# Token sums: where the first combined operands, the Relus and GpSimd's weight sums are put

## Chip, cores and metric

The kernel runs on one core of one Trainium2 chip. The metric is device time in microseconds (us). Everything is float32.

Engines are named as in the profile: PE is TensorE (matmuls; PEld its weight loads), DVE is VectorE, ACT is ScalarE, POOL is GpSimd, SP is SyncE, which here only issues DMAs. PSUM is the memory that PE writes to, in banks; SBUF holds everything else on the chip.

## What is computed

The input x has 8 images of 3008 tokens by 256 channels. A filter over the tokens is followed by a mixer over tokens and then over channels.

```python
X = np.fft.rfft(x, axis=1)
x = np.fft.irfft(X * (filt_r + 1j * filt_i)[None], n=3008, axis=1)      # filter
xt = x.transpose(0, 2, 1)
h = np.maximum(xt @ w_tok1, 0.0) @ w_tok2                               # 3008 -> 256 -> 3008
u = x + h.transpose(0, 2, 1)
h2 = np.maximum(u @ w_ch1, 0.0) @ w_ch2                                 # 256 -> 1536 -> 256
return u + h2
```

## The kernel before

**The loop.** `mix` goes through the mixer's work in 288 steps: 8 images `b`, 6 stretches of tokens `m` in each (512 tokens wide, the last 448), 6 channel pairs `jp` in each stretch. So an image has 36 steps, `i % n` from 0 to 35 with n = 36, and a step is one channel pair of one stretch. A step multiplies up to the hidden channels (`up_first`, `up_middle`, `up_last`) and, one step behind, down from them (`h_sums`, `down`). Between these, at three places of a step, come other pieces: token products for the next image, parts of `u` for the next stretch (`u_parts`), and, through the generator's yields, the filter of images that come later (`dft`, L523 on PE and L674 to L680 on DVE in its second half).

**Order.** The schedule is written by hand. Each engine works through its instructions in the order in which the program issues them, and so does each engine that issues DMAs: SP and POOL also keep the order of their DMAs. What stands earlier in the code on one engine is done earlier there.

**Seven products for eight.** All large products are done by a scheme that replaces eight block products by seven, with sums of the blocks ahead of and behind them. Weights therefore come as seven blocks: four of them raw or nearly so, others sums that `combine` forms on POOL (L378 to L382). On the side of the data, sums of the four blocks are formed on DVE: `h_sums` and `u_sums` for the channel part (tiles `t` and `v`), `t4_sums` for the token part (tile `ts`). The helper `v` issues every DVE sum, so they all carry its line, L910, and are told apart by their tiles.

**Token product.** For images 1 to 7, `token_product` (L802 on PE) forms the first token product from the filtered rows in `t4`. It runs over 12 pairs of row groups. In a pair there are 7 products, each of which is two passes on PE, into two PSUM banks called `one` and `two` (`ps_acc` and `ps_b` in the trace). Three use raw rows, four use sums in `ts`. `ts` holds two pairs of four 128 x 128 sums, so the sums of pair j + 2 are formed after pair j's products. It stands in step 32 of an image (the `n - 4` of the code), at the last of its three places, and belongs to the next image. The sums of pairs 0 and 1 are formed earlier in that step, after one piece of the delayed work of the preceding stretch (`one_step`; here it is an output transpose and the output's DMAs on POOL).

Behind the products, the same function forms the results in a tile `c`: a copy on ACT (L808), five sums on DVE, two Relus on ACT into `h1` (L815), and `combine` of `h1` on POOL. PE first uses `h1` in step 34.

**Up, in a step.** `up_first` issues four products, into four half banks, and a copy `s` of the first of them by ACT (L935). `up_middle` is two sums on DVE that read `s` and the banks, into `hh` and `s`. `up_last` issues three more products into half banks that these two sums have read, then two sums and two Relus (L953).

**Weight sums on POOL.** The weights of the token product are loaded and converted for image 0 into `w1` and used once as they are. For the later images, `w1_sums` then makes the seven blocks from them: `raw_out` stores the raw ones to DRAM by two POOL DMAs (L761, L762; 0.77 and 1.54 MB by their KB in the profile), sixteen POOL sums of 128 x 384 (L765) overwrite `w1` in place, and `sums_out` stores the four sums (L774). A list `w1_todo` holds these 18 pieces; `mix` takes two from it in each step from step 8 of image 0. `w2_sums` does the same for the second token weight (L880 to L896), one piece a step, also from step 8.

**Other work on POOL and SP in image 0.** In the first steps of image 0 the last channel weights are still converted on DVE, and `combine` finishes them on POOL (`wc`). Up to step 7 the first transform of images 1 and 2 is done (L530 on PE), with results stored through ACT's queue to `z_tmp`. At the second place of step 7, three POOL memsets clear the tiles `filt` (L694); then SP loads the filter's rows into `filt` and the transform's results into `t` (`t<-z_tmp`), in this order in its queue, and the first filter product (L523) follows in step 8.

## Time and profile before

| | us |
|---|---|
| median of 3 runs | 2470.65 (2469.56 to 2470.77) |
| profiled execution, own time | 2472.55 |
| its span, first to last instruction | 2470.8 |
| PE busy | 2409.5 (98%) |
| DVE busy | 1946.4 (79%) |
| ACT busy | 687.0 (28%) |
| POOL busy | 622.1 (25%) |

How to read it: the profile is of one execution; its span leaves out what lies around the first and the last instruction. Matmuls are pipelined and their ends are modelled, so a busy PE is not PE at its peak. POOL's 622.1 us are for the most part the issue of output DMAs (L1013, 409.6 us). In lines of the timeline the first two numbers are the start (us from the span's start) and the time from the first to the last of the merged instructions; then engine, line, operation, tiles written and read, and in brackets the idle time before it and what ended it. In lines of the waits: who waited, for whom, total us, times, longest.

### The profile page before, as it was taken

What the parts mean: (1) busy time and instruction counts of PE and PEld (TensorE: products, weight loads), DVE (VectorE), ACT (ScalarE), POOL (GpSimd) and SP (SyncE); (2) the same over time, 40 slices, a digit from 0 to 9 for tenths busy, and PEclk for the clock granted to TensorE, in tenths of its full rate; (3) what the DMA queues carried; (4) which work ended last, traced back from release to release, by engine and by line L of the source; (5) the groups of instructions that cost most, each with busy time, mean ns of one, the idle gap of its engine ahead of it and who ended that gap; (6) DMA issues with size and microseconds to landing.
All of it is one profiled execution on the core that took longest, in us unless ns stands there. A gap on an engine that the chain in (4) does not pass through costs nothing.

```text
span 2470.8 us, 35576 instructions
## 1 busy us (share of the span) xinstructions
PE 2409.5 (98%) x12340; PEld 1969.5 (80%) x12340; DVE 1946.4 (79%) x3684; ACT 687.0 (28%) x1355; POOL 622.1 (25%) x1110
## 2 busy tenths in 40 slices
PE   7999999999999999999999999999999999999998
PEld 4667666978878787987888878897888888898887
DVE  7797878787887888778877887877787788777776
ACT  5733222133221222123221222213221222212222
POOL 8473632113111211211121112112212112112121
PEclk8999999999999999999999999999999999999999
DMA  9974455453442322435334222433324121411100
GB/s 217 239 230 150 142 159 176 151 158 113 120 139 87 86 83 79 157 108 167 99 115 128 86 70 81 155 93 116 98 82 147 50 71 46 148 62 29 40 14 20
DMA packets 187339, 278.65 MB, mean 113 GB/s; under 512 B 35405, under 2 KB 125211, under 8 KB 187160
## 3 DMA queue, kind: packets, MB, share of 16 engines
q1 hardware_dynamic: 140952, 212.56, 28.4%
q0 software_dynamic: 34608, 53.83, 8.1%
q10 hardware_dynamic: 11600, 10.00, 1.3%
q8 instruction: 98, 1.61, 0.3%
q14 instruction: 81, 0.66, 0.1%
HBM read 193.52 MB, written 82.72 MB: 112 GB/s over the span
## 4 chain that ended last, share of the span: by engine, by line
PE 84%; DVE 9%; DMA 3%; issue 1%; ACT 1%; POOL 0%; SPq 0%; DVEq 0%; ACTq 0%
PE ps_po L966 31%; PE ps_pg L932 18%; PE ps_pg L948 13%; PE ps_b L523 4%; PE ps_b L802 3%; PE ps_acc L853 3%; PE ps_acc L802 2%; PE ps_b L853 2%; DVE t L910 2%; PE ps_b L831 2%; PE ps_acc L831 2%; DVE hh L910 2%; DMA st<-in_moe_w_tok_dram 1%; PE ps_acc L523 1%; DVE s L910 1%
## 5 line engine op out<-in xcount | busy, mean ns | idle before, releaser
L1013 POOL DMA_DIRECT2D out_dram<-r x752 | 409.6, 553 | 1623.3 <-ACT hh L953 1341.0
L910 DVE TENSOR_TENSOR hh<-ps_pg,s 128x512 f32<-128x512 f32 (+3 forms) x864 | 482.5, 586 | 240.0 <-ACT s L935 236.1
L953 ACT ACTIVATE hh<-hh 128x512 f32<-128x512 f32 (+1 forms) x576 | 348.0, 622 | 966.9 <-DVE hh L910 966.9
L966 PE MATMUL ps_po<-t,wc 128*128 128x256 f32 (+1 forms) x2304 | 548.2, 381 | 6.2 <-DVE t L910 4.4
L966 PEld LDWEIGHTS ps_po<-t,wc 128*128 128x128 f32 x2304 | 425.0, 190 | 136.1 <-DVE t L910 49.8
L966 PE MATMUL ps_po<-hh,wc 128*128 128x256 f32 (+1 forms) x1728 | 414.0, 375 | 1.4 <-POOL wc L382 0.8
L932 PE MATMUL ps_pg<-v,wc 128*128 128x256 f32 (+1 forms) x1728 | 413.4, 375 | 0.1
L966 PEld LDWEIGHTS ps_po<-hh,wc 128*128 128x128 f32 x1728 | 326.5, 190 | 42.7 <-ACT s L935 3.9
L932 PEld LDWEIGHTS ps_pg<-v,wc 128*128 128x128 f32 x1728 | 326.9, 190 | 40.6 <-DVE v L910 2.6
L948 PE MATMUL ps_pg<-u,wc 128*128 128x256 f32 (+1 forms) x1152 | 296.0, 379 | 6.0 <-DVE hh L910 6.0
L948 PEld LDWEIGHTS ps_pg<-u,wc 128*128 128x128 f32 x1152 | 214.3, 190 | 65.7 <-DVE hh L910 32.7
L910 DVE TENSOR_TENSOR t<-t,hh 128x256 f32<-128x256 f32 (+1 forms) x576 | 247.2, 429 | 19.8
L910 DVE TENSOR_TENSOR s<-ps_pg,hh 128x512 f32<-128x512 f32 (+1 forms) x288 | 196.1, 681 | 30.7 <-DVE hh L910 0.9
L935 ACT COPY s<-ps_pg 128x256 f32<-128x256 f32 (+1 forms) x288 | 105.9, 368 | 327.9 <-PE ps_pg L932 325.3
L910 DVE TENSOR_TENSOR t<-hh 128x512 f32<-128x512 f32 (+1 forms) x288 | 196.1, 681 | 0.6 <-ACT hh L953 0.6
L932 PE MATMUL ps_pg<-u,wc 128*128 128x256 f32 (+1 forms) x576 | 172.3, 381 | 3.9 <-DVE hh L910 3.9
L948 PE MATMUL ps_pg<-v,wc 128*128 128x256 f32 (+1 forms) x576 | 168.8, 375 | 0.0
L932 PEld LDWEIGHTS ps_pg<-u,wc 128*128 128x128 f32 x576 | 105.8, 190 | 36.8 <-DVE hh L910 21.8
L910 DVE TENSOR_TENSOR u<-ps_acc,u 128x256 f32<-128x256 f32 (+1 forms) x84 | 46.2, 550 | 94.0 <-PE ps_acc L853 86.4
L948 PEld LDWEIGHTS ps_pg<-v,wc 128*128 128x128 f32 x576 | 108.8, 190 | 13.0
L910 DVE TENSOR_TENSOR u<-ps_b,u 128x512 f32<-128x512 f32 (+2 forms) x126 | 74.5, 591 | 28.8 <-PE ps_b L853 26.7
L853 PE MATMUL ps_acc<-w 128*128 128x256 f32 (+1 forms) x336 | 85.2, 376 | 0.0
(149 smaller groups left out, 2744.6 us busy)
## 6 DMA issues: line engine op xcount, KB each, us to landing
w<-w_tmp SPq DMA_DIRECT2D x84, 448.0 KB
w<-w_tmp SPq DMA_DIRECT2D x35, 896.0 KB
out_dram<-r POOLq DMA_DIRECT2D x696, 32.0 KB, 3.1
t<-g_tmp SPq DMA_DIRECT2D x42, 512.0 KB
g_tmp<-t SPq DMA_DIRECT2D x96, 192.0 KB
t<-z_tmp SPq DMA_DIRECT2D x180, 96.0 KB
z_tmp<-t SPq DMA_DIRECT2D x60, 256.0 KB
filt<-in_x_dram SPq DMA_DIRECT2D x90, 128.0 KB
```

Of the source, the lines that this page charges most:

```text
L523: nc.tensor.matmul(outs(i, j), stat(i, j), mov(i, j), start=True, stop=True)
L802: nc.tensor.matmul(ps[:, at], w[:, n], mov, start=(j == 0 and i in (0, 2)), stop=(j == AP - 1 and i >= 5))
L831: nc.tensor.matmul(ps[:, ds(q * P, n)], t4[b, c][:, r, ts(dh, P)], wai[:, 0:n], start=(first and q == 0), stop=(not first and q == 3))
L853: nc.tensor.matmul(ps[:, ds(j * hw, hw)], h1[:, n, :], w2m[m % 2][:, at, 0:hw], start=(i < 2 and j == 0), stop=(j == len(todo) - 1))
L910: nc.vector.tensor_tensor(out=out, in0=in0, in1=in1, op=op)
L932: nc.tensor.matmul(ps[:, 0:hw], chan[0][:, jp, n, :], mov, start=True, stop=True)
L935: nc.scalar.copy(out=s[:, 0], in_=g[0][:, 0, 0:hw])
L948: nc.tensor.matmul(ps[:, 0:hw], chan[0][:, jp, n, :], mov, start=True, stop=True)
L953: nc.scalar.activation(out=hs, in_=hs, func=AF.Relu)
L966: nc.tensor.matmul(po[i][:, j, 0:hw], chan[1][:, jp, n, :], mov, start=(jp == 0 and first == 1), stop=(jp == JP - 1 and last == 1))
L1013: q.dma_start(bass.AP(tensor=ob.tensor, offset=ob.offset + row * D + g * cw, ap=[[N1 * D, 32], [D if h else -D, n], [1, cw]]), blocks[ts(g ...
```

## The change

1. In `token_product` the seven products of a pair stand in another order: the three with raw rows come first, the four with sums after them. In `mix`, `t4_sums` of pair 0 moves ahead of the delayed piece of work in step 32; that of pair 1 stays behind it.
2. The last of the five sums, the two Relus and `combine` of `h1` become a function that is put aside, and is called in the next step, after `up_first` and `up_middle`.
3. `w1_todo` is taken from at the start of a step: one piece (`raw_out`) in step 4 of image 0, six in each of steps 5, 6 and 7 (the sixth to the eighth channel pair). Nothing is left for step 8 and later.

No instruction is added or taken away.

```diff
-    token_ts = {}
+    token_ts, todo_h1 = {}, []
...
-            todo = ((one, 0, 0, rows[:, 0]), (one, 3, 6, t[:, 0]), (two, 0, 4, t[:, 1]), (one, 2, 3, t[:, 2]),
-                    (two, 1, 2, t[:, 3]), (one, 1, 1, rows[:, 2]), (two, 2, 5, rows[:, 3]))
+            todo = ((one, 0, 0, rows[:, 0]), (one, 1, 1, rows[:, 2]), (two, 2, 5, rows[:, 3]), (one, 3, 6, t[:, 0]),
+                    (two, 0, 4, t[:, 1]), (one, 2, 3, t[:, 2]), (two, 1, 2, t[:, 3]))
...
-        v(c[:, 5:7], two[:, 1:3], c[:, 3:5])
         h1 = w2[:, 0:1, 7 * 256:].rearrange("p o (s t) -> p o s t", t=P)[:, :, 0:7, :]
-        for at, to in ((slice(1, 7, 5), slice(0, 5, 4)), (slice(5, 8, 2), slice(1, 7, 5))):
-            nc.scalar.activation(out=h1[:, 0, to, :], in_=c[:, at], func=AF.Relu)
-        combine(h1)
+
+        def finish_h1():
+            v(c[:, 5:7], two[:, 1:3], c[:, 3:5])
+            for at, to in ((slice(1, 7, 5), slice(0, 5, 4)), (slice(5, 8, 2), slice(1, 7, 5))):
+                nc.scalar.activation(out=h1[:, 0, to, :], in_=c[:, at], func=AF.Relu)
+            combine(h1)
+
+        todo_h1.append(finish_h1)
         return h1[:, 0]
...
         for i in range(len(items) + 1):
             now, old = i < len(items), i >= 1
+            if JP - 2 <= i < JP + 2:
+                for _ in range(6 if i > JP - 2 else 1):
+                    if w1_todo:
+                        w1_todo.pop(0)()
...
                 s = up_first(jp, uts[b, m], vts[b, m], w, g)
                 up_middle(hhs[i], w, g, s)
+            while todo_h1:
+                todo_h1.pop()()
             one_step()
...
                 up_last(jp, uts[b, m], vts[b, m], w, g, s, hhs[i])
+                if b + 1 < B and i % n == n - 4:
+                    t4_sums(b + 1, 0)
             one_step()
             if now and i % n == n - 1:
                 one_step()
-            if now and i >= 8:
-                for _ in range(2):
-                    if w1_todo:
-                        w1_todo.pop(0)()
             if now and b + 1 < B:
                 if n - 4 - W1S <= i % n < n - 4:
                     w1_load(i % n - (n - 4 - W1S))
                 if i % n == n - 4:
-                    for j in range(2):
-                        t4_sums(b + 1, j)
+                    t4_sums(b + 1, 1)
```

## The prediction

> **What bounds the kernel now.** I read the page's busy shares first, then the waits, then the timeline around each edited place. TensorE (PE) is busy 98% of the span, so an edit is worth what it takes out of PE's idle time, or puts in. Page and waits:

> ```profile
> PE 2409.5 (98%) x12340; PEld 1969.5 (80%) x12340; DVE 1946.4 (79%) x3684; ACT 687.0 (28%) x1355; POOL 622.1 (25%) x1110
> ...
> POOL w L378 <- ACT w L815: 83.0, 7, 12.7
> ...
> PE ps_pg L948 <- DVE hh L910: 6.0, 11, 0.7
> PE ps_b L802 <- DVE ts L910: 6.0, 7, 0.9
> ```

> Columns: total us, times, longest. PE's own waits are short and recur seven times, once in each image 0 to 6, where the token sums of the next image stand. The timeline of the first such place (a step is one channel pair, counted from 0 in its image, 36 to an image; this is step 32) shows the first wait:

> ```profile
> 446.32 0.38 PE L802 MATMUL ps_b<-t,w 128*128 128x128 f32 x2
> 446.48 0.70 DVE L998 STREAM_TRANSPOSE r<-u 128x512 f32<-128x512 f32 x1
> 447.11 0.38 DVE L910 TENSOR_TENSOR ts<-t 128x256 f32<-128x256 f32 x1
> ...
> 447.63 0.46 PE L802 MATMUL ps_b<-ts,w 128*128 128x128 f32 x2 [0.93 <-DVE ts L910]
> ```

> PE does one raw product (two passes), then idles 0.93 us (0.84 in the six other places) until VectorE (DVE), which did an output transpose first, has the first combined operand. Twenty us later, step 33:

> ```profile
> 467.83 0.42 DVE L910 TENSOR_TENSOR c<-ps_acc,c 128x256 f32<-128x256 f32 x1
> 468.35 0.72 ACT L815 ACTIVATE w<-c 128x256 f32<-128x256 f32 x2 [1.86 <-DVE c L910]
> 468.98 0.33 ACT L935 COPY s<-ps_pg 128x224 f32<-128x224 f32 x1
> 469.33 0.39 DVE L910 TENSOR_TENSOR hh<-ps_pg,s 128x224 f32<-128x224 f32 x1 [1.08 <-ACT s L935]
> 469.78 1.02 PE L948 MATMUL ps_pg<-u,wc 128*128 128x224 f32 x4 [0.72 <-DVE hh L910]
> ```

> The copy of `s` stands in ScalarE's queue behind the two Relus of the token sums, which wait for DVE's last sum. DVE then waits 1.08 us for `s`, and PE 0.72 us for DVE, plus 0.13 us at 471.18. The third edit concerns GpSimd (POOL) in image 0:

> ```profile
> 213.38 0.53 POOL L694 MEMSET filt<- 128x512 f32 x1 [16.75 <-PE ps_b L530]
> ...
> 251.17 0.99 POOL L765 TENSOR_TENSOR w<-w 128x384 f32<-128x384 f32 x1 [10.05 <-DMA w_tmp<-w]
> ...
> 262.54 2.94 POOL L765 TENSOR_TENSOR w<-w 128x384 f32<-128x384 f32 x2
> 263.13 1.49 DVE L680 TENSOR_TENSOR p<-p,p 128x512 f32<-128x512 f32 x1
> 263.36 1.04 PE L523 MATMUL ps_b<-p,wb 64*64 64x512 f32 x2 [0.99 <-DVE p L679]
> ```

> L765 are the weight sums. While they run, a DVE operation of two SBUF inputs takes 1.49 us (281.29, with POOL idle: 0.68), and PE waits.

> [...] `t<-hh` 128x512 goes from 0.68 to 1.50 us beside L765, while a pair of `hh<-ps_pg,s` (one input in PSUM) stays at 1.28. [...] for the two raw stores (2.36 MB) [...] the trace shows 10.05 us of waiting behind them[...], at 87% DMA share. [...] beside the raw stores SP's loads took 0.9 to 1.3 us each to issue, against 0.23 to 0.37 at 227 to 237.

> **Edit 1: raw products first, sums of pair 0 ahead of the transpose.** Counts are unchanged: 168 passes and 36 DVE sums an image. Step 32 of images 2, 4 and 6 lasts 25.17 us; twelve pairs at 1.56 (first pass of pair 1 at 448.49, of pair 2 at 450.05) are 18.72; the same step of image 7, with no token sums, is 5.30 (2436.05 to 2441.35). Lost: 1.15. New: three raw products are six passes of 0.111, so PE needs a sum at 446.99. DVE is free at 446.48 and has the first at 446.86, visible some 0.07 later. The transpose moves behind pair 0's three sums, so pair 1's sums start at 448.06 as now and arrive at 448.55; PE wants them at 446.32 + 1.56 + 0.67 = 448.55. No wait to speak of. Later pairs: a sum's buffer is freed two products later and needed two later, ten products between as before. The store behind the transpose moves 0.95 us later on a POOL queue that idled 23.87 us before it, and `r` is next written at 466: nothing. I take 1.0 of 1.15 (bounds 0.6 to 1.15).

> **Edit 2: last sum, Relus and h1's sums behind the next step's copy.** Step 33 (images 2, 4, 6) is 6.72 us against 5.30 in image 7: 1.42 lost. New: `s` is copied about 1.05 us after the step's first matmul (480.10 to 481.11 elsewhere), at 467.3; DVE ends its four `c` operations at 468.25 and starts `hh` at 468.27, not 469.33. Behind it come `s` (0.62), the last `c` sum (0.42), `t` (0.58 + 0.82), two `hh` (1.15): the first `hh` ends near 472.0 and PE can start step 34 at 472.04, not 472.97: 0.93. DVE is the limit there, so some 0.4 us of loss stays. Who waits for the moved work: h1's sums on POOL begin near 470.6 instead of 469.16; the fourth is ready 2.4 us later, 473.1, and PE's first use in step 34 is near 474.7. Margin 1.5, so no wait. The banks held longer are next written in step 34, or, in images 1, 3 and 5, at the end of step 33. I take 0.95 (bounds 0.3 to 1.3).

> Edits 1 and 2: 7 x 1.95 = 13.7 us.

> **Edit 3: weight sums in steps 5 to 7 instead of 8 to 16.** Removed: step 12 lasts 10.91 us against 8.21 for step 18 with the same matmuls, step 13 7.91 against 7.26 (19), 14 9.38 against 9.16 (20), 16 15.54 against 12.48 (22). Together 6.6 us; the w2 sums (L880, L891) stay, so I take 5.5 (bounds 3 to 6.6). Added: the raw stores (1.07 + 1.03 us to issue) enter POOL's queue before the last two `wc` combinations, at about 189.7; those end near 194.7 and 197.2, and PE wants them after 200.2 and 208.8: nothing. The stores land near 201 (9.5 us: DMA share is 25 to 44% there). Sixteen L765 at about 1.1 us run to 218.6, the last store is issued till 219.7, and only then come the three memsets, which were at 213.4 and 219.8. SP's filter loads wait for memset 0, and the z loads `t<-z_tmp` (223.5 now) stand behind them in SP's queue. The first filter product, step 8, already waits on its loads: 8.33 us against 7.26 for step 11. The last store (L774, 3.1 MB, which filled the DMA engines from 308 to 316) now lies over exactly these loads, which I put at 3 us more for PE (bounds 0 to 8). DVE slowed in steps 5 to 7: it is busy 4.9 of 10 us from 195 to 215, 7.5 from 215 to 225; I take 1.5 (bounds 0.3 to 4). Slower z stores and x loads beside the raw stores: 0.5 (0 to 1.5). Net: 5.5 - 5.0 = +0.5 (bounds -8 to +6).

> **Sum.** 13.7 + 0.5 = 14.2 us. The profiled execution took 2472.55 us (span 2470.8 and 1.75 around it): 2458.35. The median of the runs is 1.9 lower, 2470.65; the forecast beside it is 2456.5.

> **Rivals.** (a) *Edits 1 and 2 work, edit 3 costs*: L765 slower[...], or the stores landing at 204, push the memsets to 224 and the z loads to 229 to 235; PE stalls 8 us in step 8. 13.7 + 5.5 - 8, less 4 for DVE slowed in steps 5 to 7, is 7.2: 2463.5. For: POOL and SP queues are in order, and step 8 has no slack. Against: memset 0 has some 9 us of cover (213.4 to 222.8) before the z loads move. (b) *Edit 3 pays nearly in full*, 4.5 net: 2452.5. For: steps 5 and 6 have half-idle DVE. (c) *The token edits give half*, because step 33 is bound by DVE's own chain or PE's gap only moves to pair 1, where I find no slack at all: 6.8 + 0.5, 2463.3. (d) *Slower*: the same POOL queue as in (a) becomes the bound of image 0. Every us of memset 0 beyond 222.8 is a us of PE. It decides when the stall passes 13.7 + 5.5 = 19.2 us, memset 0 at 242: that takes L765 at 2.4 us each, twice the 1.145 mean seen. A stall of 25 us would give 2476.5. (e) *It does not do what it says*: for edit 1 only if DVE took the sums no earlier, which an in-order queue excludes.

> **How the numbers follow.** About 0.2% (4.9 us) is what a measurement of this kernel can tell from no change. Forecast 0.62, own range 2454 to 2460; (a) 0.14; (b) 0.11; (c) 0.08; (d) 0.05. Half of (a) and (c) lie below 2463.5; with (b)'s lower half left out, 2451.5 to 2464 holds eight in ten. Faster by over 0.2% is below 2465.7: forecast, (b), most of (a) and (c): 0.90. Within 0.2%: 0.05. Slower: 0.05.

> **What would show it.** Right: `ps_b<-ts` gone from PE's waits; in step 33 `s` copied ahead of `w<-c`, PE's 0.72 gone and `hh` starting right behind the fourth `c`; step 32 near 24.2, step 33 near 5.8; L765 between 201 and 219; step 12 near 8.3, step 16 near 12.6. Step 8 between 9 and 14 us tells how much of edit 3 comes back as a wait. Wrong: PE waiting in pair 1 or for h1's sums in step 34, or memset 0 past 226.

## The result and the profile after

| | us |
|---|---|
| before, median (4 runs) | 2470.71 (2469.56 to 2472.95) |
| after, median (4 runs) | 2455.16 (2454.31 to 2458.64) |
| ratio, 95% interval | 0.9939 (0.9921 to 0.9956) |
| profiled executions, span | 2470.8 before, 2453.8 after |

The changed kernel is faster by 15.5 us, 0.6%. The forecast was 2456.5 us. The total fits; its parts do not, and the experiments show why. In the kernel after, the lines from `t4_sums` on have moved by 4 (L910 is L914, L966 is L970, and so on; L1013 is L1017).

The busy shares and PE's own waits after (who waited, for whom, total us, times, longest):

```profile
PE 2402.2 (98%) x12340; PEld 1973.3 (80%) x12340; DVE 1937.0 (79%) x3684; ACT 687.3 (28%) x1355; POOL 620.9 (25%) x1110
```

```profile
PE ps_b L523 <- DMA t<-z_tmp: 7.2, 1, 7.2
...
PE ps_pg L936 <- DVE hh L914: 3.9, 4, 2.1
PE ps_po L970 <- DVE t L914: 3.8, 8, 0.6
...
PE ps_b L523 <- DVE p L679: 0.9, 2, 0.4
```

Two rows of seven waits are gone: `ps_b L802` for `ts`, and those of step 33 in `ps_pg` for `hh` (their row, `ps_pg` L948 before and L952 here, has gone from 6.0 to 0.7 us). The waits of L523 for `p` have shrunk from 3.5 to 0.9 us. A new wait has come, once, and it is the longest in the mixer: the first filter product waits 7.2 us for its loads.

The timeline of step 32 of image 0, where the token product starts (in the steps shown, bank `one` is `ps_b` and `two` is `ps_acc`):

```profile
447.18 0.61 PE L802 MATMUL ps_b<-t,w 128*128 128x128 f32 x4
447.34 0.42 DVE L914 TENSOR_TENSOR ts<-t 128x256 f32<-128x256 f32 x1
447.62 0.39 PE L802 MATMUL ps_acc<-t,w 128*128 128x128 f32 x2
...
447.90 0.46 PE L802 MATMUL ps_b<-ts,w 128*128 128x128 f32 x2
```

Three raw products (six passes) run while DVE forms the first sum, and the first product with a sum has no wait before it. Step 33:

```profile
467.08 0.35 ACT L939 COPY s<-ps_pg 128x224 f32<-128x224 f32 x1 [0.77 <-PE ps_pg L936]
467.19 0.42 DVE L914 TENSOR_TENSOR c<-ps_b,c 128x256 f32<-128x256 f32 x1
...
467.53 0.38 DVE L914 TENSOR_TENSOR hh<-ps_pg,s 128x224 f32<-128x224 f32 x1
...
468.56 0.41 DVE L914 TENSOR_TENSOR c<-ps_acc,c 128x256 f32<-128x256 f32 x1
468.71 0.92 PE L952 MATMUL ps_pg<-u,wc 128*128 128x224 f32 x4
...
469.07 0.72 ACT L817 ACTIVATE w<-c 128x256 f32<-128x256 f32 x2 [1.64 <-DVE c L914]
```

`s` is copied 2 us before the Relus, `hh` follows DVE's third sum of `c` at once, and PE has no idle time before L952. The third edit, on POOL, with SP's loads behind it (`SPq` is SP's queue):

```profile
198.52 18.29 POOL L765 TENSOR_TENSOR w<-w 128x384 f32<-128x384 f32 x16 [4.16 <-DMA w_tmp<-w]
217.11 1.08 POOL L774 DMA_DIRECT2D w_tmp<-w  x1 [0.30 <-POOL w L765]
218.19 1.47 POOL L694 MEMSET filt<- 128x512 f32 x3
```

```profile
219.11 1.25 SPq L228 DMA_DIRECT2D filt<-in_filt_r_dram  x1
...
228.00 0.30 SPq L631 DMA_DIRECT2D t<-z_tmp  x1
...
232.67 2.35 PE L523 MATMUL ps_b<-t,wb 48*64 48x512 f32 x4 [7.23 <-DMA t<-z_tmp]
234.38 2.37 PE L523 MATMUL ps_acc<-t,wb 48*64 48x512 f32 x4
...
236.68 3.60 PE L970 MATMUL ps_po<-t,wc 128*128 128x256 f32 x8
```

The same place before:

```profile
223.50 0.30 SPq L631 DMA_DIRECT2D t<-z_tmp  x1
...
227.04 1.07 PE L523 MATMUL ps_b<-t,wb 48*64 48x512 f32 x4
227.79 1.41 PE L523 MATMUL ps_acc<-t,wb 48*64 48x512 f32 x4
...
229.13 1.99 PE L966 MATMUL ps_po<-t,wc 128*128 128x256 f32 x8
```

The z loads were issued from 223.5 before; here from 228.0. And PE is slow after its wait: eight passes of L970 take 3.60 us against 1.99 before. The view by stages shows the clock of PE there (columns: stretch, its length, busy us of PE, PEld, DVE, ACT, POOL, then the granted clock of PE, DMA share, GB/s):

```profile
226.00:228.00 2.00, 0.00 (x0) 0.00 (x0) 1.57 (x3) 1.23 (x2) 0.00 (x0) 1.00 0.98 359
228.00:230.00 2.00, 0.00 (x0) 0.00 (x0) 0.00 (x0) 0.00 (x0) 1.79 (x4) 0.93 0.43 120
230.00:232.00 2.00, 0.00 (x0) 0.00 (x0) 0.00 (x0) 0.00 (x0) 2.00 (x4) 0.50 0.55 139
...
236.00:238.00 2.00, 2.00 (x5) 1.15 (x4) 1.56 (x2) 0.00 (x0) 2.00 (x4) 0.50 0.53 138
238.00:240.00 2.00, 2.00 (x6) 1.55 (x6) 1.30 (x3) 0.00 (x0) 0.02 (x1) 0.51 0.80 279
```

While PE idles, its clock goes to 0.50 (at 229.72 in the trace), and it stays there until 239.96, 10.24 us.

Where the time went, by steps (start of one step's first product to the next one's, both traces):

| steps | before to after, us | difference |
|---|---|---|
| ahead of step 0 | 143.83 to 140.96 | -2.9 |
| 4 to 7 of image 0 | steps 4, 6, 7: +0.11, +0.33, +0.81 | +1.2 |
| 8 of image 0 | 8.33 to 19.15 | +10.8 |
| 12, 13, 14, 16, 18 of image 0 | 10.91 to 7.51, 7.91 to 7.26, 9.38 to 9.14, 15.54 to 12.48, 8.21 to 7.44 | -8.1 |
| 32 of images 0 to 6 | 25.17 to 24.15 (images 2, 4, 6) | -7.2 |
| 33 of images 0 to 6 | 6.72 to 5.30 (images 2, 4, 6) | -10.2 |
| 34 of images 0, 2, 4, 6 | 7.13 to 7.02 | -0.4 |

The rows add up to -16.8; between the spans it is 16.94. So, by the steps of these two traces, the token edits gave 17.8 us and the weight sums cost 3.9. The change does not touch what stands ahead of step 0: there the traces differ from run to run (step 0 starts between 138.2 and 144.7 in those shown here), so those 2.9 us are not put down to it.

### The profile page after: what moved, and what is told of

The parts are those of the page before. It is cut to its first block, busy times and chain, and to the rows that moved or that the text cites. A ratio compares the mean times of both kernels' runs of the same rounds, so it can differ in the third digit from the quotient of the medians.

```text
span 2453.8 us, 35566 instructions
## 1 busy us (share of the span) xinstructions
PE 2402.2 (98%) x12340; PEld 1973.3 (80%) x12340; DVE 1937.0 (79%) x3684; ACT 687.3 (28%) x1355; POOL 620.9 (25%) x1110
## 4 chain that ended last, share of the span: by engine, by line
PE 87%; DVE 6%; DMA 3%; issue 1%; ACT 1%; POOL 1%; SPq 0%; ACTq 0%; DVEq 0%; POOLq 0%
PE ps_po L970 33%; PE ps_pg L936 18%; PE ps_pg L952 14%; PE ps_b L523 5%; PE ps_b L802 3%; PE ps_acc L857 3%; PE ps_acc L802 2%; PE ps_b L857 2%; PE ps_b L835 2%; PE ps_acc L835 2%; DVE t L914 1%; PE ps_acc L523 1%; DVE hh L914 1%; PE ps_b L751 1%; DVE u L914 1%
## 5 line engine op out<-in xcount | busy, mean ns | idle before, releaser
L1017 POOL DMA_DIRECT2D out_dram<-r x752 | 409.5, 553 | 1647.4 <-ACT hh L957 1135.5
L914 DVE TENSOR_TENSOR hh<-ps_pg,s 128x512 f32<-128x512 f32 (+3 forms) x864 | 481.6, 585 | 233.3 <-ACT s L939 230.7
L970 PE MATMUL ps_po<-t,wc 128*128 128x256 f32 (+1 forms) x2304 | 548.1, 381 | 4.7 <-DVE t L914 3.8
L970 PEld LDWEIGHTS ps_po<-t,wc 128*128 128x128 f32 x2304 | 427.5, 190 | 131.5 <-DVE t L914 44.2
L970 PE MATMUL ps_po<-hh,wc 128*128 128x256 f32 (+1 forms) x1728 | 414.0, 375 | 1.4 <-POOL wc L382 0.8
L970 PEld LDWEIGHTS ps_po<-hh,wc 128*128 128x128 f32 x1728 | 326.5, 190 | 42.9 <-ACT s L939 3.6
L952 PE MATMUL ps_pg<-u,wc 128*128 128x256 f32 (+1 forms) x1152 | 295.2, 379 | 0.7 <-DVE hh L914 0.7
L914 DVE TENSOR_TENSOR t<-t,hh 128x256 f32<-128x256 f32 (+1 forms) x576 | 246.6, 428 | 19.8
L952 PEld LDWEIGHTS ps_pg<-u,wc 128*128 128x128 f32 x1152 | 214.9, 190 | 57.6 <-DVE hh L914 25.1
L914 DVE TENSOR_TENSOR s<-ps_pg,hh 128x512 f32<-128x512 f32 (+1 forms) x288 | 196.0, 681 | 30.7 <-DVE hh L914 0.9
L914 DVE TENSOR_TENSOR t<-hh 128x512 f32<-128x512 f32 (+1 forms) x288 | 193.4, 672 | 0.6 <-ACT hh L957 0.6
L952 PE MATMUL ps_pg<-v,wc 128*128 128x256 f32 (+1 forms) x576 | 168.8, 375 | 0.0
L914 DVE TENSOR_TENSOR u<-ps_acc,u 128x256 f32<-128x256 f32 (+1 forms) x84 | 46.2, 550 | 93.9 <-PE ps_acc L857 86.5
L952 PEld LDWEIGHTS ps_pg<-v,wc 128*128 128x128 f32 x576 | 109.2, 190 | 12.5
L914 DVE TENSOR_TENSOR u<-ps_b,u 128x512 f32<-128x512 f32 (+2 forms) x126 | 74.4, 591 | 28.9 <-PE ps_b L857 26.7
```

The costliest lines, as they stand in the source:

```text
L914: nc.vector.tensor_tensor(out=out, in0=in0, in1=in1, op=op)
L952: nc.tensor.matmul(ps[:, 0:hw], chan[0][:, jp, n, :], mov, start=True, stop=True)
L970: nc.tensor.matmul(po[i][:, j, 0:hw], chan[1][:, jp, n, :], mov, start=(jp == 0 and first == 1), stop=(jp == JP - 1 and last == 1))
L1017: q.dma_start(bass.AP(tensor=ob.tensor, offset=ob.offset + row * D + g * cw, ap=[[N1 * D, 32], [D if h else -D, n], [1, cw]]), blocks[ts(g ...
```

## Experiments

Beside experiments 1 to 3 and the half store of experiment 4, 17 runs of the kernel before lay between 2467.33 and 2474.98, median 2470.79. The quarter store has 7 of its own (median 2474.12). Experiments 5 to 7 have one run each, beside one of the kernel before at 2473.01, and are read from their traces, step by step.

**1. The token edits alone.**

```diff
-            if JP - 2 <= i < JP + 2:
-                for _ in range(6 if i > JP - 2 else 1):
...
+            if now and i >= 8:
+                for _ in range(2):
...
```

> The change without its third edit: the token product's new order and the last sum, Relus and h1's sums put off, but the weight sums back in steps 8 to 16. My theory (the token edits save 2.5 us in each of seven images, and the third edit as it stands costs 3 to 4 us): 2470.7 - 17.5 = 2453, some 2 us below the changed kernel's 2455.2; step 8 back at 8.3, step 12 at 10.9 and step 16 at 15.5. The rival of my prediction (the weight sums pay a little, the token edits give less): slower than the changed kernel, 2456 to 2459.

Measured: 2455.38 us (2452.69 to 2457.51), ratio 0.9936 (0.9923 to 0.9948). Steps 32 and 33 are those of the changed kernel, to 0.02 us. Step 8 is 8.97, step 12 is 11.91, step 16 as before. So the first two edits give all of the gain, and the third makes no difference that these runs tell. The interval (2451.8 to 2457.9 us) takes in the 2453 of the theory and most of its rival's 2456 to 2459, so the times do not decide between them. In this trace steps 8 and 12 took more than in the one trace of before (8.97 and 11.91 against 8.33 and 10.91).

**2. The weight sums alone.**

```diff
+            if JP - 2 <= i < JP + 2:
+                for _ in range(6 if i > JP - 2 else 1):
...
-            if now and i >= 8:
-                for _ in range(2):
...
```

> The kernel before with the third edit alone. By the steps of the two traces the third edit is +12.1 us in steps 4 to 8 and -8.1 in steps 12 to 18: slower by 3 to 4 us, about 2474.5. If it is worth what the prediction said: 2470. If the token edits and the weight sums act on each other (they are 170 us apart, so I do not expect it), the sum of this difference and that of the token edits alone does not give the changed kernel's.

Measured: 2472.84 us (12 runs, 2471.62 to 2474.74), ratio 1.0008 (0.9999 to 1.0016): 2 us slower by the medians, an interval that just takes in no change, where 3 to 4 us slower was expected. In its trace step 8 is 18.89 and steps 12 to 18 lose the same 8.1 us, and steps 32 and 33 are those of the kernel before: no sign that the two parts act on each other. The two differences by the medians add up to -13.4 us against the changed kernel's -15.5, which these runs do not tell apart.

**3. The store of the sums put off to step 9.**

```diff
-                    if w1_todo:
+                    if len(w1_todo) > 1:
                         w1_todo.pop(0)()
+            if i == JP + 3:
+                w1_todo.pop(0)()
```

> The changed kernel, with the store of the weight sums alone (3.1 MB) put off from step 7 to step 9; raw stores and the sixteen sums stay in steps 4 to 7, so the memsets still come after the sums. If that store, lying over the filter's first loads, is what makes step 8 last 19.15 us: step 8 falls to 8.5 to 9.5, the time to about 2445. If the late memsets behind the sums (217 instead of 213) and SP's order are the cause: step 8 stays above 14 and the time above 2450.

Measured: 2446.32 us (2444.03 to 2447.31), ratio to before 0.9897 (0.9884 to 0.9911), clear of the changed kernel's interval: this version beats both. Step 8 is 7.76, below even the 8.5 to 9.5 that was expected. POOL and SP in its trace, then PE:

```profile
217.79 1.59 POOL L694 MEMSET filt<- 128x512 f32 x3
```

```profile
218.71 0.36 SPq L228 DMA_DIRECT2D filt<-in_filt_r_dram  x1
...
221.98 0.30 SPq L631 DMA_DIRECT2D t<-z_tmp  x1
```

```profile
226.41 0.65 PE L523 MATMUL ps_b<-t,wb 48*64 48x512 f32 x2
...
227.92 1.99 PE L970 MATMUL ps_po<-t,wc 128*128 128x256 f32 x8
```

The memsets are as late as in the changed kernel (218.19), and it does no harm. What has gone is the store beside SP's loads: they issue in 0.23 to 0.38 us each (in the changed kernel five of the eight took 1.04 to 1.25), and the z loads come 6 us earlier (221.98 against 228.00). Three MB moved from step 7 to step 9 are worth 9 us by the medians, and 11.4 in step 8 of the traces.

**4. Half of the store, and a quarter of it, left in step 7.** The store is cut in two by pairs of row groups, the first part in step 7, the rest in step 9 by the edit of experiment 3. The quarter's code; the half cuts at 6:

```diff
+        def sums_out(j, k):
+            return lambda: nc.gpsimd.dma_start(to[:, j:k, 3:7], w[:, j:k].rearrange("p j r t n -> p j (r t) n"))
...
+        return todo + [sums_out(0, 3), sums_out(3, AP)]
```

> As the one before, but half of the store (1.6 MB) stays in step 7 and half goes to step 9. If PE's stall in step 8 follows the length of the store: step 8 near 13 to 14, about 2449.5. If any store there costs the whole stall by its place in the queues: step 8 near 19, 2455. If the stall comes from the last part of the store alone: step 8 near 9, 2445.

Half: 2453.68 us, ratio 0.9929 (0.9915 to 0.9942); step 8 is 15.89, neither 13 to 14 nor 19. PE's gap is 4.17 us, and the clock is at 0.50 from 231.96 for 6.83 us. In SP's queue one filter load waits 2.4 us for an earlier one to land.

```profile
231.77 2.16 PE L523 MATMUL ps_b<-t,wb 48*64 48x512 f32 x4 [4.17 <-DMA t<-z_tmp]
...
235.66 3.52 PE L970 MATMUL ps_po<-t,wc 128*128 128x256 f32 x8
```

So the gap follows the length of the store roughly (7.23, 4.17), and time at half clock comes on top of it. Is there a length of the gap from which it does?

> A quarter of the weight sums' store (0.8 MB) in step 7, the rest in step 9. The half store left PE idle for 4.17 us and its clock was granted at 0.50 for some 7 us after that; the whole store 7.23 us. If the cost of step 8 is the idle time[...]: the gap here is 1 to 2.5 us, the clock stays at 1.00 and step 8 lasts 9 to 10.5 us, the time 2447.5 to 2449. If any wait there costs the half clock: step 8 above 12, 2451 or more.

Quarter: 2449.82 us, ratio 0.9911 (0.9893 to 0.9929). Step 8 is 13.30, and the expectation failed: the gap was in its range, and the clock fell all the same (to 0.50 for 6.83 us from 225.67).

```profile
225.15 1.96 PE L523 MATMUL ps_b<-t,wb 48*64 48x512 f32 x4 [1.71 <-DMA t<-z_tmp]
226.47 2.27 PE L523 MATMUL ps_acc<-t,wb 48*64 48x512 f32 x4
...
228.68 3.78 PE L970 MATMUL ps_po<-t,wc 128*128 128x256 f32 x8
```

A gap of 1.71 us cost 5.5 us over the 7.76 of the version without a store there. It isn't any delay, though: in the trace of before L523 and L966 take 3.92 us here, 1.07 more than in an undisturbed step, and the clock stays at 1.00. The last section looks at what stood ahead of each fall in all traces.

**5. The sums left out.** The token edits alone, and no L765:

```diff
-            todo += [pool(c22, c21, c22, ALU.add), pool(c21, c11, c21, ALU.subtract),
-                     pool(c11, c22, c11, ALU.subtract), pool(c12, c12, c11, ALU.subtract)]
+            todo += [lambda: None] * 4
```

> The token edits alone, weight sums where they were (steps 8 to 16), but the sixteen sums on GpSimd are left out; their stores stay. If those sums hold VectorE's two-input operations up and so PE: step 12 falls from 11 to about 7.5, step 16 from 15.5 to 12.5, VectorE's t<-hh back at 0.68 us, the time near 2446. If the stores' traffic costs these steps: step 16 stays near 15.5, the time near 2453.

Measured: 2448.75 us, one run. Step 16 falls to 12.48 and step 12 to 8.63 (15.55 and 11.91 in experiment 1). Step 12 does not reach the 7.5 that was expected: without the sums POOL runs through its queue earlier, and w2 sums (L883, L894), from 253.23 to 257.03, now lie in step 11, where `t<-hh` at 255.23 takes 1.21 us instead of 0.68 and DVE's work runs on into step 12. So what slowed these steps is POOL's sums beside DVE, not the stores: the store of the sums still begins in step 16 (at 297.57, the step is 293.19 to 305.67), which has lost its 3 us all the same.

**6. The first edit in its two halves.** The order of the products without the sums' new place, and the reverse, both with the weight sums in steps 8 to 16 as in experiment 1:

```diff
-                if b + 1 < B and i % n == n - 4:
-                    t4_sums(b + 1, 0)
...
-                    t4_sums(b + 1, 1)
+                    for j in range(2):
+                        t4_sums(b + 1, j)
```

> Weight sums in steps 8 to 16; of the first edit only the order of the seven products, with the sums of pair 0 still behind the transpose. PE then wants a sum 0.67 us after its first pass, and VectorE has it some 1.24 us after: a wait of 0.5 to 0.6 instead of 0.84, step 32 near 24.8 (images 2, 4, 6; 25.17 before, 24.15 with both). If the order alone does it: 24.15. If it does nothing alone: 25.17.

Measured: step 32 of images 2, 4, 6 at 24.73 (24.72 in 4 and 6), PE's gap 0.49 in image 0, near what was expected (2456.80 us).

```diff
-            todo = ((one, 0, 0, rows[:, 0]), (one, 1, 1, rows[:, 2]), (two, 2, 5, rows[:, 3]), (one, 3, 6, t[:, 0]),
+            todo = ((one, 0, 0, rows[:, 0]), (one, 3, 6, t[:, 0]), (two, 0, 4, t[:, 1]), (one, 2, 3, t[:, 2]),
...
```

> Weight sums in steps 8 to 16; of the first edit only the sums of pair 0 ahead of the transpose, the seven products in their old order. The first sum comes 0.6 us after PE's first pass and PE wants it after 0.22: a wait of 0.3 to 0.4, step 32 near 24.6. If the place of the sums alone does it: 24.15. If the wait only moves to pair 1, behind the transpose: above 24.9.

Measured: 24.59 to 24.60, gap 0.34, as expected (2456.39 us). Each half takes 0.45 to 0.58 off, and together they take 1.02: two shifts of one wait, which add up until the wait is gone.

**7. The second edit without its sum.** The last sum of `c` stays where it was; Relus and h1's sums are put off. The weight sums are in steps 8 to 16.

```diff
-        def finish_h1():
-            v(c[:, 5:7], two[:, 1:3], c[:, 3:5])
+        v(c[:, 5:7], two[:, 1:3], c[:, 3:5])
+
+        def finish_h1():
```

> Weight sums in steps 8 to 16; of the second edit only the Relus and h1's sums are put off, the last sum of c stays ahead of the next step's sums on VectorE. If the copy behind the Relus was the wait: step 33 near 5.4 (6.72 before, 5.30 with the sum put off too), as VectorE has the same work in another order. If VectorE's chain ahead of hh decides, as the prediction reckoned it: near 5.8.

Measured: 2454.22 us; step 33 at 5.40 in images 2 and 4, as expected from the copy. In images 1, 3 and 5, where a filter step shares it, it is 7.60, 7.60 and 6.65, against 6.88, 6.88 and 5.98 with the sum put off too (experiment 1). Image 1, with the sum kept:

```profile
754.37 0.42 DVE L915 TENSOR_TENSOR c<-ps_acc,c 128x256 f32<-128x256 f32 x1
754.71 0.38 DVE L915 TENSOR_TENSOR hh<-ps_pg,s 128x224 f32<-128x224 f32 x1
...
755.70 0.53 POOL L378 TENSOR_SCALAR w<-w 128x128 f32<-128x128 f32 x1 [9.93 <-ACT w L818]
...
757.52 0.94 DVE L679 TENSOR_TENSOR p<-p,p 128x512 f32<-128x512 f32 x1
...
758.60 1.41 PE L523 MATMUL ps_b<-p,wb 64*64 64x512 f32 x3 [0.30 <-DVE p L679]
```

The same in experiment 1, with the sum put off (the step starts at 758.16 there, at 752.78 above):

```profile
759.63 0.38 DVE L914 TENSOR_TENSOR hh<-ps_pg,s 128x224 f32<-128x224 f32 x1
...
761.99 0.53 POOL L378 TENSOR_SCALAR w<-w 128x128 f32<-128x128 f32 x1 [11.26 <-ACT w L817]
762.44 0.68 DVE L679 TENSOR_TENSOR p<-p,p 128x512 f32<-128x512 f32 x1
```

The copy ahead of the Relus gives 1.32 of the 1.42 us; the sum behind gives the rest, and 0.7 us where DVE has the filter's work too. DVE has the same work in both, so its order alone does not explain these 0.7 us. The sum kept ahead also lets POOL begin h1's sums 0.9 us earlier in the step, and beside them three DVE operations with both inputs in SBUF take longer than in experiment 1: `t<-hh` 0.73 against 0.61, the pair `t<-t,hh` 1.09 against 0.88, the first `p<-p,p` 0.94 against 0.68. That is 0.6 of the 0.7.

## Why the prediction was right or wrong

**What bounds.** Right for the token edits: PE's waits were the measure, and the two seven-fold waits went. For the weight sums they were not all: PE's clock, at 0.50 for 10.24 us, counted too.

**Edit 1**, 1.0 forecast: 1.02 to 1.04 a step. The wait did not move to pair 1, although no slack was seen there. Rival (c) falls for this edit, and for the next; so does (e), since DVE took the sums earlier.

**Edit 2**, 0.95 forecast: 1.42 to 1.52. The step that failed is the count of DVE's sums. The text has "its four `c` operations" ahead of `hh` and "the last `c` sum" behind it, five in all, and the description of the kernel says five; the code has four. The fourth, at 467.83 in the trace of before, is the last one, which moves. So `hh` starts 1.47 us after the step's first product (466.06 to 467.53), not 2.03, DVE has 0.42 us less to do than was reckoned, and no loss stays. POOL's sums of h1 came in time: no wait in step 34, which even gained 0.1.

**Edit 3**, +0.5 forecast: -3.9 by the steps of the traces. The times tell less: experiment 1 and the changed kernel do not differ (2455.38 and 2455.16), and experiment 2 is between nothing and 4 us slower than before. What was taken away was sized too low: 8.1 us against 5.5, outside the bounds, since step 18, taken as the reference, was itself slowed and fell by 0.77. Steps 4 to 7 cost 1.2 against 2.0 for the two terms. The order on POOL came as described, even sooner: sums from 198.5, memsets at 218.2, not 219.7. The step that failed is "which I put at 3 us more for PE (bounds 0 to 8)": step 8 grew by 10.8, and its 19.15 us are also outside the 9 to 14 named at the end. By the traces this has two parts. The first filter product came 11.71 us into the step instead of 4.41: 7.3 more, the wait for the loads. From there to the end of the step, L523 and L970 took 7.44 us, nearly all at half clock, instead of 3.92 at full clock: 3.5 more (an undisturbed step of 7.26 has 2.85 for them). Of these, 1.6 us are L970's eight passes alone (3.60 against 1.99); in L523's share, a wait of PE's weight loads for later data (1.00 us before 234.34) and the clock are not told apart. The first part lay in the bounds. The second had no term at all. The trace of before has such a case: ahead of L751 PE waits 2.65 us for `t<-g_tmp`, to 113.38, and its clock is at 0.50 from 113.60 to 117.02. So a stall of 3 to 8 us should have been priced with it. How long a wait has to be for it was not shown there; the quarter store's 1.71 us were followed by half clock too (last section).

Rival (a) had the place right, and with 8 us nearly the length of the wait, but not the reason: it was not the late memsets, which experiment 3 keeps, but the store behind the sums, to which the forecast itself gave 3 us. Rival (b)'s gain in steps 12 to 18 was there and went back in step 8. Rival (d) is far off: the loss stopped at 10.8 us.

**The sum** was 14.2 us and the medians gave 15.5. That it fits is luck in part: by the steps of the traces two errors met, 4 us too little for the token edits and 4 too much for the weight sums.

## What to carry to other kernels

A large store that nobody waits for was not free here: with 3.1 MB beside the loads for PE step 8 took 19.15 us, without it 7.76. Look for a place for it where no queue has just begun to load for PE. Before a wait on TensorE is priced, ask what its clock does then: here a wait of 7.23 us came with 10.24 us at 0.50. And where one trace shows an ACT or DVE instruction at the head of a queue with the critical one behind it, count the instructions by name in the code as well as in the trace before the new order is reckoned.

## What the runs showed of the hardware

POOL's sums beside DVE have no simple price either: the same sixteen took 18.3 us in steps 5 to 7 and, with the stores, slowed PE by 1.2 us in steps 4 to 7; in steps 12 to 18 they and what they pushed back cost 8.1. In the trace of before DVE was busy 17.3 of 30 us from 195 to 225, and 60.1 of 68 from 259 to 327, its slowed operations included. That DVE's slack in a step decides how much of the slowing reaches PE fits these figures, but no run varied it alone.
